# A fused S5 scan and GEGLU block on one core: another order for D's row, the parameters, C and slab 2 on the load queue

## The chip, the core and the metric

The kernel runs on one core of a Trainium2 chip. A core has five engines that run side by side: PE (TensorE, products of matrices), DVE (VectorE), ACT (ScalarE), POOL (GpSimd) and SP (SyncE, which here only issues transfers). The metric is the device time of one execution in microseconds (us). Four executions of the kernel before took 180.09 to 180.79 us, with a median of 180.47 us.

## The reference

```python
def reference(x, Lambda_re, Lambda_im, B_re, B_im, C_re, C_im, log_dt, Dskip, w_gate, w_up, w_down):
    xn = layernorm(x)                                   # x: 2048 x 512, bf16
    Lam = Lambda_re + 1j * Lambda_im                    # 512 states
    dt = exp(log_dt);  Lam_bar = exp(dt * Lam)
    B_bar = ((Lam_bar - 1) / Lam)[:, None] * (B_re + 1j * B_im)
    h_t = Lam_bar * h_{t-1} + B_bar @ xn_t              # over the 2048 tokens
    s = 2 * Re(h @ C.T) + xn * Dskip
    g = silu((gelu(xn @ w_gate) * (xn @ w_up)) @ w_down)    # w_gate, w_up: 512 x 1376
    return x + s * g
```

## The kernel before

The 2048 tokens are handled in four slabs of 512, and each slab in four tiles of 128 tokens. For every slab PE does four kinds of products: gate and up (`gate_tile`, line L530, for slabs 1 to 3, and `GatePair`, L501, for slab 0, where the 1376 columns come in three pieces as the weights land), the inputs of the scan (`inputs`, L638, against `BT`), the down product (`down_pair`, L573, against `wd`, with the gated activations turned by a DMA into `atT`), and the output of the scan (`y_tile`, L601, against `C2`).

Around them, ACT takes the results out of PSUM (`gt`, `ub`, `U`, `g`), with three table sets for its functions, and each change of set is an ACT_TABLE_LOAD. DVE multiplies gate and up into `at`, rotates the scan's inputs with tables of sines, runs the scan (TENSOR_TENSOR_SCAN, L675), and rotates back into `hst`. PSUM is cut into three slots of two banks (`slots`), which gate, up, inputs and down take in turn, and two single banks (`ybank`).

Every operation is first recorded as a step of a `Plan`, with an estimated cost and its dependencies. The plan then searches for an order and emits each engine's instructions in it. PE's steps are chained in the order of the program text; the other engines' steps may be moved by the planner, unless `after=` or `in_turn` ties them. Each engine then executes its own list strictly in order, and an instruction that waits holds up all that stand behind it.

Three places matter here.

The head. Small loads on ACT's queue bring three parameter vectors into `pv` and D's row (1 x 512) into `Drow[0:1]`. `dummies` are products of ones that keep PE busy. `columns` turns eight parameter rows into columns by one product with the identity (L393). `head_t(m)` turns the centred tile m of slab 0 on PE (L445), and ACT or DVE copies the result into `W` (L448, L449), which is the left operand of the first gate products. `spread` copies D's row to all 128 partitions: a product of one row of ones with `Drow[0:1]` (L748), and an ACT copy back into `Drow` (L749). `sines` makes the tables' sines (L705, L706). `damping` turns the third parameter vector with a product of its own (L739) and a DVE copy (L740).

The load queue. SP issues all large transfers. `dma_first` chains some of them; the rest stand where the planner puts them. In the kernel before, the order after slab 0's weights is: the transposing load of C's real part (L362), the transposition of slab 1 into `xnT` (L366), `wd` (L893), x of slab 2 (L872), the last rows of `wd` (L894), the transpositions of slab 0's `at` tiles 0 to 2 (L556), the transposing load of C's imaginary part (L362), `at` tile 3 (L556), and x of slab 3. Each `at` tile is turned into 11 blocks of `atT`, and the down product of tile m waits for the blocks of that tile.

C's scaling and slab 2's statistics. `tF` is C scaled by a coefficient on ACT (L897, four pieces), and DVE makes `C2` of it (L899, L902), which waits for both parts of C. Slab 2's mean and mean square are made on ACT (L876, eight steps), which waits for x of slab 2.

Of the kernel before, what the change touches and what calls it, by code (L numbers as in the profile page):

```python
# [202 lines left out]
def kernel(  # L203
# [46 lines left out]
    def sb(name, shape, dt=BF16):  # L250
        return consts.tile(shape, dt, name=name)
# [5 lines left out]
    wd = sb("wd", [P, NFT, D])  # L257
    BT = sb("BT", [P, 2, KT, D])
    C2 = sb("C2", [P, 2, NPT, D])
    pv = [sb("pv0", [2 * NPT, P]), sb("pv1", [NPT, P])]  # L260
    Drow = sb("Drow", [P, D])
    hst = [sb(f"hst{i}", [P, 2, NPT, TS]) for i in range(2)]
    CT = hst[1]
# [38 lines left out]
    def pe(n, cols, emit, reads=(), writes=(), **kw):  # L302
        return pl.add(PE, n * (cols + 6) / 2400.0, emit, reads, writes, lag=0.22, **kw)
# [4 lines left out]
    def dma(eng, issue, land, emit, reads=(), writes=(), **kw):  # L308
        return pl.add(eng, issue, emit, reads, writes, lag=land, **kw)
# [21 lines left out]
    def load_x(eng, q, m, land):  # L331
        dma_first(eng, 0.45, land, lambda: q.dma_start(out=x_tok[:, m, :], in_=x_r[:, m, :]), [("x", 0, m)], not_before=0.72)

    load_p(0, A_log_dt, pv[0][0:NPT, :])
    load_p(1, A_Lambda_im, pv[0][NPT : 2 * NPT, :])
    behind = [first[ACT]]
    load_p(2, A_Lambda_re, pv[1][:])
    dma(ACT, 0.4, 3.0, lambda: nc.scalar.dma_start(out=Drow[0:1, :], in_=A_Dskip.rearrange("(a d) -> a d", a=1)), writes=["Drow"], after=[first[ACT]], rank=-20.0)
    def load_first(c, which, land):
        load_w(dma_first, SP, nc.sync, c, (1.45 * (CH0[c][1] - CH0[c][0]) / 512, land), which)  # L340

# [19 lines left out]
    def load_c(ri):  # L361
        dma_first(SP, 1.9, 4.0, lambda: nc.sync.dma_start_transpose(out=CT[:, ri, :, :], in_=(A_C_re, A_C_im)[ri]), [("CT", ri)])  # L362

    def turn_slab(s, land, after=()):

# [20 lines left out]
    acts(1, lambda: act(out=tiny[:], in_=zero[:], func=AF.Exp), ["zero"], ["tiny"], table="exp", rank=150.0, after=behind)  # L386
    pf = small("pf", 16)
    dt_, thn, lim, lre = (pf[:, 4 * i : 4 * i + 4] for i in range(4))
    rows = slots[2][:, 0, 0 : 2 * NPT]

    def columns():

        pe(1, 150, lambda: T.matmul(rows, lhsT=pv[0][:], rhs=ident[0 : 2 * NPT, 0 : 2 * NPT], start=True, stop=True),  # L393
            [("pv", 0), ("pv", 1), "ident"], [("slot", 2, 0)])
        acts(4, lambda: act(out=dt_, in_=rows[:, 0:NPT], func=AF.Exp), [("slot", 2, 0), "tiny"], ["dt"], table="exp", rank=150.0)
# [123 lines left out]
    def gate_tile(s, m):  # L519
# [24 lines left out]
        for kind, (nm, wt, dst) in enumerate((("wg", wg, gt[q]), ("wu", wu, ub[q]))):  # L544
# [5 lines left out]
        dve(b - a, lambda: V.tensor_tensor(out=at[j][:, a:b], in0=gt[q][:, a:b], in1=ub[q][:, a:b], op=ALU.mult),  # L550
            [("gtb", q), ("ubb", q)], [("at", j, 2)], rate=2.0)

    def at_t(s, m, c0, c1):
        j = (s * M + m) % NAT
        k0, k1 = CK[c0][0], CK[c1][1]
        dma(SP, 1.3, 2.2, lambda: nc.sync.dma_start_transpose(  # L556
            out=atT[:, k0:k1, m * P : (m + 1) * P], in_=at[j][:, k0 * P : k1 * P]),
            [("at", j, c) for c in range(c0, c1 + 1)] + [("atpad", j)], [("atT", m, c) for c in range(c0, c1 + 1)])

    g2s = {}  # L560
    g2_n = [0]
# [142 lines left out]
    def sines():  # L704
        early.append(acts(196, lambda: act(out=sbt[:], in_=ang[:], func=AF.Sin, scale=TWO_PI), ["ang"], ["sbt"], table="silu", rank=20.0))  # L705
        early.append(acts(196, lambda: act(out=cbt[:], in_=kr[:], func=AF.Sin, scale=-TWO_PI, bias=halfpi[:]), ["kr", "halfpi"], ["cbt", "trig"], table="silu", rank=20.0))  # L706

    def tables(behind):
        NB4 = [P, NPT, NA, NB // 2, 2]
# [25 lines left out]

    def damping():

        ps = ybank[0][:, 0:NPT]
        pe(1, 150, lambda: T.matmul(ps, lhsT=pv[1][:], rhs=ident[0:NPT, 0:NPT], start=True, stop=True), [("pv", 2), "ident"], [("y", 0)])  # L739
        dve(4, lambda: V.tensor_copy(out=lre, in_=ps), [("y", 0)], ["lre"], base=0.14)  # L740
        dve(4, lambda: V.tensor_tensor(out=a1[:], in0=lre, in1=dt_, op=ALU.mult), ["lre", "dt"], ["a1"])
        power(rho[:], e_t[:], a1[:], 4, ["a1", "e_t"], ["rho"])

    def head_t(m, evict):
        return transposed(xc[m], xcT[:, m], [("xc", m), ("F", m // 2, m % 2)], [("xcT", m)], m % 2, evict)

    def spread():
        pe(1, 512, lambda: T.matmul(slots[2][:, 1, :], lhsT=warm[0:1, 0:P], rhs=Drow[0:1, :], start=True, stop=True), ["Drow", "warm"], [("slot", 2, 1)])  # L748
# [47 lines left out]
    pairs[2].products(1)  # L796
    pairs[3].products(0)
    pairs[3].products(1)
    gelus = [p.close() for p in pairs]
    tables(gelus[:1])  # L800
    load_rest()
# [10 lines left out]
        gate_pairs(m, 1)  # L812
    for h in range(2):
        half(0, h)
    for m in range(M):
# [44 lines left out]
    def norm1():  # L860
        for m in range(M):
            stats(1, m)
            mean(1, m)
        rstd(1, 0, M)
        for m in range(M):
            norm_dve(1, m)
        first[SP] = turn_slab(1, 3.0, [first[SP]])
        for m in range(M):
            skip(1, m)

    def norm_act(s):
        dma(SP, 0.5, 4.0, lambda: nc.sync.dma_start(out=x_tok[:, s * M : (s + 1) * M, :], in_=x_r[:, s * M : (s + 1) * M, :]),  # L872
            writes=[("x", s, m) for m in range(M)], not_before=(30.0, 50.0)[s - 2], rank=40.0)
        for m in range(M):
            for i, fn in enumerate((AF.Copy, AF.Square)):
                acts(512, lambda i=i, fn=fn, m=m: act(out=junk[:], in_=x_tok[:, s * M + m, :], func=fn, accum_out=sx[:, s, i, m : m + 1]),  # L876
                     [("x", s, m)], ["junk", ("sx", s, i, m)], ptr=2)
        mean, var = sx[:, s, 0, :], sx[:, s, 1, :]

        def f():  # L880
            V.tensor_scalar(out=mean, in0=mean, scalar1=1.0 / D, scalar2=None, op0=ALU.mult)
            V.tensor_tensor(out=mq[:, s, :], in0=mean, in1=mean, op=ALU.mult)
            V.tensor_scalar(out=var, in0=var, scalar1=1.0 / D, scalar2=EPS, op0=ALU.mult, op1=ALU.add)
            V.tensor_tensor(out=var, in0=var, in1=mq[:, s, :], op=ALU.subtract)
        pl.add(DVE, 0.35, f, [("sx", s, i, m) for i in range(2) for m in range(M)], [("var", s)], lag=0.13)
        power(rs[:, s, :], var, mhalf[:], M, [("var", s), "mhalf"], [("rs", s, m) for m in range(M)])
        dve(M, lambda: V.scalar_tensor_tensor(out=nb[:, s, :], in0=mean, scalar=-1.0, in1=rs[:, s, :], op0=ALU.mult, op1=ALU.mult),
            [("var", s)] + [("rs", s, m) for m in range(M)], [("nb", s)])
        for m in range(M):
            norm_out(s, m)  # L890

    norm1()
    dma_first(SP, 3.6, 4.3, lambda: nc.sync.dma_start(out=wd[:, 0 : NFT - 1, :], in_=B_w_down[0 : (NFT - 1) * P, :].rearrange("(k p) d -> p k d", p=P)), ["wd"])  # L893
    dma_first(SP, 0.4, 4.3, lambda: nc.sync.dma_start(out=wd[:FL, NFT - 1, :], in_=B_w_down[(NFT - 1) * P : F, :]), ["wd"])  # L894
    load_c(1)
    for pt in range(NPT):
        acts(1024, lambda pt=pt: act(out=tF[:, :, :], in_=CT[:, :, pt, :], func=AF.Copy, scale=cim[:, pt : pt + 1]),  # L897
             ["coef", ("CT", 0), ("CT", 1)], [("tF",)], ptr=1)
# [67 lines left out]
```

## Time and profile before

| what | value |
|---|---|
| four executions | 180.79, 180.19, 180.75, 180.09 us; median 180.47 us |
| the profiled execution | 180.79 us, of which 179.0 us are the span from the first to the last instruction |
| PE busy | 173.6 us (97% of the span), 852 products |
| DVE busy | 157.9 us (88%) |
| ACT busy | 119.3 us (67%) |
| POOL busy | 8.0 us (4%) |
| mean granted TensorE clock | 0.999 |
| moved by DMA | 18.53 MB, 104 GB/s on average |

The span leaves out some 1.8 us of the profiled execution (180.79 less 179.0). The table of forty slices (4.5 us each) shows PE at nine tenths or more from the second slice to the last but one, with a single 8 in the eleventh. DVE is as full from the fourth slice to the thirty-fourth. The DMA engines are full from the second slice to the tenth, that is to 45 us, and have pauses after the eleventh. Only the waits of the engine that sets the end cost time. A wait of one that is ahead costs nothing, until it makes that engine late.

### The profile page before, as it was taken

To read this page: it belongs to the slowest core of one execution; us is meant where nothing else is said; L and a number is where in the kernel's file an instruction comes from. 1 tells how busy PE (TensorE), PEld (TensorE's weight loads), DVE (VectorE), ACT (ScalarE), POOL (GpSimd) and SP (SyncE) were. 2 spreads that over 40 slices of the span, in tenths; PEclk is the share of its full clock that TensorE was granted. 3 is DMA by queue.
4 is the path that set the end of the run, shared out by engine and by line. 5 is a ranking of instruction groups with operands and counts; after the bars stand their busy time and mean duration, and the time that the engine had idled before them with its cause. 6 is when DMAs were issued, how large, how long until landed. Compare 5 with 4: busy or idle time off the path is not lost.

```text
span 179.0 us, 2401 instructions
## 1 busy us (share of the span) xinstructions
PE 173.6 (97%) x852; PEld 82.4 (46%) x852; DVE 157.9 (88%) x268; ACT 119.3 (67%) x180; POOL 8.0 (4%) x17
## 2 busy tenths in 40 slices
PE   7999999999899999999999999999999999999992
PEld 2454444444344445444445554544445555444451
DVE  4989999999999999999999999999999999860063
ACT  3899989678999988938259864554518666353220
POOL 2120023000002000000020000000000000000000
PEclk9999999999999999999999999999999999999999
DMA  5999999999700479400011665141100344420011
GB/s 144 322 243 209 310 114 190 354 232 216 118 0 0 84 139 140 81 29 2 0 59 36 111 135 105 36 81 33 60 0 0 72 82 93 97 72 29 0 58 59
DMA packets 49093, 18.53 MB, mean 104 GB/s; under 512 B 40409, under 2 KB 49082, under 8 KB 49082
## 3 DMA queue, kind: packets, MB, share of 16 engines
q1 hardware_dynamic: 49056, 18.39, 47.9%
q8 instruction: 6, 0.10, 0.2%
q14 instruction: 5, 0.04, 0.1%
q10 hardware_dynamic: 26, 0.00, 0.0%
HBM read 6.33 MB, written 2.10 MB: 47 GB/s over the span
## 4 chain that ended last, share of the span: by engine, by line
PE 70%; DVE 15%; DMA 8%; ACT 3%; SPq 1%; issue 1%; DVEq 0%
PE slot L530 31%; PE slot L573 17%; PE ybank L601 14%; PE slot L638 8%; DMA x_tok<-in_A_x_dram 4%; DMA atT<-at 3%; DVE Fs L675 3%; DVE Q L656 3%; DVE st L420 2%; DVE at L516 1%; DVE Q L725 1%; SPq L362 1%; DMA out_dram<-ot 1%; DVE sk L473 1%; DVE ot L606 1%
## 5 line engine op out<-in xcount | busy, mean ns | idle before, releaser
L530 PEld LDWEIGHTS <-xnT 128*128 128x128 bf16 x288 | 28.2, 98 | 28.4
L573 PE MATMUL slot<-wd,atT 128*128 128x512 bf16 (+1 forms) x176 | 38.9, 379 | 0.5 <-DMA atT<-at 0.5
L530 PE MATMUL slot<-wg,xnT 128*128 128x512 bf16 (+1 forms) x144 | 31.8, 357 | 0.0
L530 PE MATMUL slot<-wu,xnT 128*128 128x512 bf16 (+1 forms) x144 | 31.8, 357 | 0.0
L675 DVE TENSOR_TENSOR_SCAN Fs<-rho,ini,W 128x512 bf16<-128x512 f32 x24 | 29.3, 1267 | 0.1
L638 PE MATMUL slot<-xnT,BT 128*128 128x512 bf16 x128 | 28.6, 379 | 0.0
L601 PE MATMUL ybank<-C,hst 128*128 128x512 bf16 (+1 forms) x128 | 28.2, 372 | 0.0
L573 PEld LDWEIGHTS <-atT 128*128 128x128 bf16 (+1 forms) x176 | 17.1, 98 | 21.6 <-DMA atT<-at 1.0
L604 DVE TENSOR_TENSOR yg<-ybank,g 128x512 bf16<-128x512 f32 (+1 forms) x16 | 10.7, 668 | 12.7 <-PE ybank L601 12.6
L641 ACT ACTIVATE U<-slot 128x1024 bf16<-128x1024 f32 x16 | 16.0, 1017 | 8.0 <-PE slot L638 8.0
L577 ACT ACTIVATE g<-slot 128x1024 f32<-128x1024 f32 x8 | 8.2, 1023 | 17.3 <-PE slot L573 17.3
L601 PEld LDWEIGHTS <-hst 128*128 128x128 bf16 x136 | 13.3, 98 | 13.8
L638 PEld LDWEIGHTS <-BT 128*128 128x128 bf16 x128 | 12.5, 98 | 15.1
L656 DVE TENSOR_TENSOR Q<-U,tab 128x4096 bf16<-128x4096 bf16 x8 | 18.3, 2287 | 0.3
L656 DVE TENSOR_TENSOR Q<-Fs,tab 128x4096 bf16<-128x4096 bf16 x8 | 18.3, 2286 | 0.1
L538 ACT ACTIVATE gt<-slot 128x1024 bf16<-128x1024 f32 x12 | 12.3, 1024 | 7.1 <-PE slot L530 5.4
L597 ACT ACTIVATE ybank<-sk 128x512 f32<-128x512 bf16 (+1 forms) x16 | 9.3, 586 | 9.2 <-DVE yg L604 9.2
L538 ACT ACTIVATE ub<-slot 128x1024 bf16<-128x1024 f32 x12 | 12.3, 1023 | 3.3 <-PE slot L530 3.0
L876 ACT ACTIVATE junk<-x_tok 128x512 bf16<-128x512 bf16 x16 | 10.1, 628 | 1.5 <-DMA x_tok<-in_A_x_dram 1.3
L675 DVE TENSOR_TENSOR_SCAN Fs<-rho,W 128x512 bf16<-128x512 f32 x8 | 9.2, 1207 | 0.0
L548 DVE TENSOR_TENSOR at<-gt,ub 128x1024 bf16<-128x1024 bf16 x12 | 8.2, 685 | 0.3 <-ACT ub L538 0.2
L501 PEld LDWEIGHTS <-W 128*128 128x128 bf16 x64 | 5.9, 98 | 5.5 <-DVE W L449 0.3
(122 smaller groups left out, 182.4 us busy)
## 6 DMA issues: line engine op xcount, KB each, us to landing
out_dram<-ot SPq DMA_DIRECT2D x15, 128.0 KB, 1.7
x_tok<-in_A_x_dram SPq DMA_DIRECT2D x3, 512.0 KB, 6.0
wd<-in_B_w_down_dram SPq DMA_DIRECT2D x1, 1280.0 KB
x_tok<-in_A_x_dram SPq DMA_DIRECT2D x4, 128.0 KB, 2.8
wg<-in_B_w_gate_dram SPq DMA_DIRECT2D x1, 512.0 KB
wu<-in_B_w_up_dram SPq DMA_DIRECT2D x1, 512.0 KB, 6.5
wg<-in_B_w_gate_dram SPq DMA_DIRECT2D x1, 480.0 KB
wu<-in_B_w_up_dram SPq DMA_DIRECT2D x1, 480.0 KB, 7.8
```

The lines of the kernel that those rows point to most:

```text
L530: T.matmul(ps[:, bank, 0 : b - a], lhsT=xnT[s % 2][:, m, k, :], rhs=wt[:, k, a:b], start=(k == 0), stop=(k == KT - 1))
L538: acts(1024, lambda ps=ps, dst=dst, fn=fn: act(out=dst[:, 0:1024].rearrange("p (c w) -> p c w", c=2), in_=ps[:, :, :], func=fn), [("slot", ...
L548: dve(1024, lambda: V.tensor_tensor(out=at[j][:, 0:1024], in0=gt[q][:, 0:1024], in1=ub[q][:, 0:1024], op=ALU.mult), qs[0] + qs[1], [("at", ...
L573: T.matmul(ps[:, b, :], lhsT=atT[:fs, k, m * P : (m + 1) * P], rhs=wd[:fs, k, :], start=(k == 0), stop=(k == NFT - 1))
L597: acts(w, lambda: act(out=bank, in_=sk[s % 2][:, m, a:z], func=AF.Copy), [("sk", s % 2, m)], [key])
L601: T.matmul(bank, lhsT=hst[s % 2][:, j // NPT, j % NPT, m * P : (m + 1) * P], rhs=C2[:, j // NPT, j % NPT, a:z], start=False, stop=(j == 2 ...
L604: dve(w, lambda: V.tensor_tensor(out=yg[e][:, a:z], in0=bank, in1=g2[gi][:, b, a:z], op=ALU.mult), [key, ("g2", gi)], [("yg", e, a)], base ...
L638: T.matmul(ps[:, ri, :], lhsT=BT[:, ri, k, pt * P : (pt + 1) * P], rhs=xnT[s % 2][:, :, k, :], start=(k == 0), stop=(k == KT - 1))
L641: acts(1024, lambda q=q, ps=ps: act(out=U[ui][:, :, q, :], in_=ps[:, :, :], func=AF.Copy), [("slot", i, 0), ("slot", i, 1)], [("U", ui, q)])
L656: dve(4096, lambda: V.tensor_tensor(out=Qf, in0=src.unsqueeze(1).to_broadcast(WQ), in1=table, op=ALU.mult), reads, ["Q"], rate=2.0)
L675: pl.add(DVE, 1.116 if s == 0 else 1.19, lambda ri=ri, q=q, pt=pt, first=first: V.tensor_tensor_scan(out=Fs[:, ri, q, :], data0=rho[:, pt ...
L876: acts(512, lambda i=i, fn=fn, m=m: act(out=junk[:], in_=x_tok[:, s * M + m, :], func=fn, accum_out=sx[:, s, i, m : m + 1]), [("x", s, m)] ...
```

## The change

D's row is spread by a product over all 128 rows (`Drow` is set to zero first, then row 0 is loaded), placed between the first two PE transpositions in the stead of one of the dummies. All three parameter vectors lie in one tile and are turned by one product; `damping` keeps only its DVE and POOL steps, and is placed later in the text. C's imaginary part is loaded right behind the real part, ahead of slab 1's transposition. Slab 1's normalisation and `wd` stand earlier in the text. The `at` transpositions are tied to one another in order, and the load of x for slab 2 is tied between the first and the second of them. The sines are tied behind the copy of the third turned tile. The planner orders the rest anew.

```diff
-    pv = [sb("pv0", [2 * NPT, P]), sb("pv1", [NPT, P])]
+    pv = sb("pv", [3 * NPT, P])
...
-    load_p(0, A_log_dt, pv[0][0:NPT, :])
-    load_p(1, A_Lambda_im, pv[0][NPT : 2 * NPT, :])
-    behind = [first[ACT]]
-    load_p(2, A_Lambda_re, pv[1][:])
-    dma(ACT, 0.4, 3.0, lambda: nc.scalar.dma_start(out=Drow[0:1, :], in_=A_Dskip.rearrange("(a d) -> a d", a=1)), writes=["Drow"], after=[first[ACT]], rank=-20.0)
+    for i, v in enumerate((A_log_dt, A_Lambda_im, A_Lambda_re)):
+        load_p(i, v, pv[i * NPT : (i + 1) * NPT, :])
...
+    dve(256, lambda: V.memset(Drow[:], 0.0), writes=["Drow"], not_before=0.72, rank=275.0)
+    dma(ACT, 0.4, 2.5, lambda: nc.scalar.dma_start(out=Drow[0:1, :], in_=A_Dskip.rearrange("(a d) -> a d", a=1)), writes=["Drow"], after=[first[ACT]], rank=-20.0)
...
-        load_c(0)
+        for ri, src in enumerate((A_C_re, A_C_im)):
+            dma_first(SP, 1.9, 4.5, lambda ri=ri, src=src: nc.sync.dma_start_transpose(out=CT[:, ri, :, :], in_=src), [("CT", ri)])
...
-    rows = slots[2][:, 0, 0 : 2 * NPT]
+    rows = slots[0][:, 1, 0 : 3 * NPT]
...
-        pe(1, 150, lambda: T.matmul(rows, lhsT=pv[0][:], rhs=ident[0 : 2 * NPT, 0 : 2 * NPT], start=True, stop=True),
+        pe(1, 150, lambda: T.matmul(rows, lhsT=pv[:], rhs=ident[0 : 3 * NPT, 0 : 3 * NPT], start=True, stop=True),
...
-        dve(4, lambda: V.tensor_copy(out=lim, in_=rows[:, NPT : 2 * NPT]), [("slot", 2, 0)], ["lim"], base=0.14)
+        dve(8, lambda: V.tensor_copy(out=pf[:, 2 * NPT :], in_=rows[:, NPT:]), [("slot", 0, 1)], ["lim", "lre"], base=0.14)
...
     def at_t(s, m, c0, c1):
...
-        dma(SP, 1.3, 2.2, lambda: nc.sync.dma_start_transpose(
+        turned[s, m] = dma(SP, 1.3, 2.2, lambda: nc.sync.dma_start_transpose(
...
+            after=[turned[s, m - 1]] if m else [first[SP]] if s == 0 else [])
...
     def damping():
-        ps = ybank[0][:, 0:NPT]
-        pe(1, 150, lambda: T.matmul(ps, lhsT=pv[1][:], rhs=ident[0:NPT, 0:NPT], start=True, stop=True), [("pv", 2), "ident"], [("y", 0)])
-        dve(4, lambda: V.tensor_copy(out=lre, in_=ps), [("y", 0)], ["lre"], base=0.14)
...
     def spread():
-        pe(1, 512, lambda: T.matmul(slots[2][:, 1, :], lhsT=warm[0:1, 0:P], rhs=Drow[0:1, :], start=True, stop=True), ["Drow", "warm"], [("slot", 2, 1)])
+        pe(1, 512, lambda: T.matmul(slots[2][:, 1, :], lhsT=warm[:, 0:P], rhs=Drow[:], start=True, stop=True), ["Drow", "warm"], [("slot", 2, 1)])
...
-    dummies(1, 0)
+    dummies(1, 1)
...
     head_t(0, ACT)
-    dummies(2, 0)
+    dummies(1, 1)
+    spread()
     behind = [head_t(1, ACT)]
...
-    sines()
...
     pairs[0].products(0)
-    spread()
     pairs[1].products(0)
     pairs[0].products(1)
-    head_t(2, ACT)
+    sines([head_t(2, ACT)])
     pairs[1].products(1)
-    damping()
...
     pairs[3].products(1)
+    damping()
...
     for h in range(2):
         half(0, h)
+    norm1()
+    dma_first(SP, 3.6, 4.3, lambda: nc.sync.dma_start(out=wd[:, 0 : NFT - 1, :], in_=B_w_down[0 : (NFT - 1) * P, :].rearrange("(k p) d -> p k d", p=P)), ["wd"])
+    dma_first(SP, 0.4, 4.3, lambda: nc.sync.dma_start(out=wd[:FL, NFT - 1, :], in_=B_w_down[(NFT - 1) * P : F, :]), ["wd"])
+    def load_slab(s, after=()):
+        return dma(SP, 0.5, 4.0, lambda: nc.sync.dma_start(out=x_tok[:, s * M : (s + 1) * M, :], in_=x_r[:, s * M : (s + 1) * M, :]),
+            writes=[("x", s, m) for m in range(M)], not_before=(30.0, 50.0)[s - 2], after=after)
     for m in range(M):
         gate_pairs(m, 2)
         at_t(0, m, 0, 2)
+        if m == 0:
+            turned[0, 0] = load_slab(2, [turned[0, 0]])
...
-    norm1()
...
-    load_c(1)
```

In the changed kernel as built, SP's list after the real part of C reads: imaginary part of C, slab 1's transposition, `wd`, the last rows of `wd`, `at` tile 0, x of slab 2, `at` tiles 1, 2 and 3, x of slab 3. ACT's list at the start of the down product reads: two copies `U`, three of slab 2's statistics, two copies `U`, the first `tF`, five statistics, the second `tF`, a table load, both `g`, a table load, the first `gt` of slab 1. On DVE, two of slab 0's four 512 wide `at` products stand ahead of slab 1's statistics in the kernel before and one in the changed kernel; the fourth of them stands just ahead of the first rotation there.

More of the change, by code (lines that the diff above doesn't have):

```diff
@@ L332, in load_x @@
         dma_first(eng, 0.45, land, lambda: q.dma_start(out=x_tok[:, m, :], in_=x_r[:, m, :]), [("x", 0, m)], not_before=0.72)
-    load_p(0, A_log_dt, pv[0][0:NPT, :])
-    load_p(1, A_Lambda_im, pv[0][NPT : 2 * NPT, :])
-    behind = [first[ACT]]
-    load_p(2, A_Lambda_re, pv[1][:])
-    dma(ACT, 0.4, 3.0, lambda: nc.scalar.dma_start(out=Drow[0:1, :], in_=A_Dskip.rearrange("(a d) -> a d", a=1)), writes=["Drow"], after=[first[ACT]], rank=-20.0)
+    behind = []
+    for i, v in enumerate((A_log_dt, A_Lambda_im, A_Lambda_re)):
+        load_p(i, v, pv[i * NPT : (i + 1) * NPT, :])
+        if i == 1:
+            behind = [first[ACT]]
+    dve(256, lambda: V.memset(Drow[:], 0.0), writes=["Drow"], not_before=0.72, rank=275.0)
+    dma(ACT, 0.4, 2.5, lambda: nc.scalar.dma_start(out=Drow[0:1, :], in_=A_Dskip.rearrange("(a d) -> a d", a=1)), writes=["Drow"], after=[first[ACT]], rank=-20.0)
     def load_first(c, which, land):
@@ L358, in load_rest @@
             load_w(dma_first, SP, nc.sync, 2, (1.35, 3.5), which)
-        load_c(0)
-    def load_c(ri):
-        dma_first(SP, 1.9, 4.0, lambda: nc.sync.dma_start_transpose(out=CT[:, ri, :, :], in_=(A_C_re, A_C_im)[ri]), [("CT", ri)])
+        for ri, src in enumerate((A_C_re, A_C_im)):
+            dma_first(SP, 1.9, 4.5, lambda ri=ri, src=src: nc.sync.dma_start_transpose(out=CT[:, ri, :, :], in_=src), [("CT", ri)])
     def turn_slab(s, land, after=()):
@@ L388 @@
     dt_, thn, lim, lre = (pf[:, 4 * i : 4 * i + 4] for i in range(4))
-    rows = slots[2][:, 0, 0 : 2 * NPT]
+    rows = slots[0][:, 1, 0 : 3 * NPT]
     def columns():
-        pe(1, 150, lambda: T.matmul(rows, lhsT=pv[0][:], rhs=ident[0 : 2 * NPT, 0 : 2 * NPT], start=True, stop=True),
-            [("pv", 0), ("pv", 1), "ident"], [("slot", 2, 0)])
-        acts(4, lambda: act(out=dt_, in_=rows[:, 0:NPT], func=AF.Exp), [("slot", 2, 0), "tiny"], ["dt"], table="exp", rank=150.0)
+        pe(1, 150, lambda: T.matmul(rows, lhsT=pv[:], rhs=ident[0 : 3 * NPT, 0 : 3 * NPT], start=True, stop=True),
+            [("pv", 0), ("pv", 1), ("pv", 2), "ident"], [("slot", 0, 1)])
+        acts(4, lambda: act(out=dt_, in_=rows[:, 0:NPT], func=AF.Exp), [("slot", 0, 1), "tiny"], ["dt"], table="exp", rank=150.0)
     def turn_angles():
-        dve(4, lambda: V.tensor_copy(out=lim, in_=rows[:, NPT : 2 * NPT]), [("slot", 2, 0)], ["lim"], base=0.14)
+        dve(8, lambda: V.tensor_copy(out=pf[:, 2 * NPT :], in_=rows[:, NPT:]), [("slot", 0, 1)], ["lim", "lre"], base=0.14)
         dve(4, lambda: V.tensor_tensor(out=thn, in0=lim, in1=dt_, op=ALU.mult), ["lim", "dt"], ["thn"])
@@ L551, in gate_tile @@
             [("gtb", q), ("ubb", q)], [("at", j, 2)], rate=2.0)
+    turned = {}
     def at_t(s, m, c0, c1):
@@ L555, in at_t @@
         k0, k1 = CK[c0][0], CK[c1][1]
-        dma(SP, 1.3, 2.2, lambda: nc.sync.dma_start_transpose(
+        turned[s, m] = dma(SP, 1.3, 2.2, lambda: nc.sync.dma_start_transpose(
             out=atT[:, k0:k1, m * P : (m + 1) * P], in_=at[j][:, k0 * P : k1 * P]),
-            [("at", j, c) for c in range(c0, c1 + 1)] + [("atpad", j)], [("atT", m, c) for c in range(c0, c1 + 1)])
+            [("at", j, c) for c in range(c0, c1 + 1)] + [("atpad", j)], [("atT", m, c) for c in range(c0, c1 + 1)],
+            after=[turned[s, m - 1]] if m else [first[SP]] if s == 0 else [])
     g2s = {}
@@ L702, in angle, with sines @@
             dve(196, lambda: V.scalar_tensor_tensor(out=kr[:], in0=ang[:], scalar=-1.0, in1=ang[:], op0=ALU.mult, op1=ALU.max), ["ang"], ["kr"], base=0.13)
-    def sines():
-        early.append(acts(196, lambda: act(out=sbt[:], in_=ang[:], func=AF.Sin, scale=TWO_PI), ["ang"], ["sbt"], table="silu", rank=20.0))
-        early.append(acts(196, lambda: act(out=cbt[:], in_=kr[:], func=AF.Sin, scale=-TWO_PI, bias=halfpi[:]), ["kr", "halfpi"], ["cbt", "trig"], table="silu", rank=20.0))
+    def sines(behind):
+        early.append(acts(196, lambda: act(out=sbt[:], in_=ang[:], func=AF.Sin, scale=TWO_PI), ["ang"], ["sbt"], table="silu", rank=20.0, after=behind))
+        early.append(acts(196, lambda: act(out=cbt[:], in_=kr[:], func=AF.Sin, scale=-TWO_PI, bias=halfpi[:]), ["kr", "halfpi"], ["cbt", "trig"], table="silu", rank=20.0, after=behind))
     def tables(behind):
@@ L814, with norm1 @@
         half(0, h)
+    def norm1():
+        for m in range(M):
+            stats(1, m)
+            mean(1, m)
+        rstd(1, 0, M)
+        for m in range(M):
+            norm_dve(1, m)
+        first[SP] = turn_slab(1, 3.0, [first[SP]])
+        for m in range(M):
+            skip(1, m)
+    norm1()
[4 more added lines that the diff above has]
+            writes=[("x", s, m) for m in range(M)], not_before=(30.0, 50.0)[s - 2], after=after)
     for m in range(M):
@@ L858, in norm_out @@
         dma(SP, 1.2, 1.3, lambda: nc.sync.dma_start_transpose(out=xnT[s % 2][:, m, :, :], in_=xn[m]), [("xn", m)], [("xnT", s % 2, m)])
[L860 to L869, printed above, removed]
     def norm_act(s):
-        dma(SP, 0.5, 4.0, lambda: nc.sync.dma_start(out=x_tok[:, s * M : (s + 1) * M, :], in_=x_r[:, s * M : (s + 1) * M, :]),
-            writes=[("x", s, m) for m in range(M)], not_before=(30.0, 50.0)[s - 2], rank=40.0)
+        if s > 2:
+            load_slab(s)
         for m in range(M):
@@ L890, in norm_act @@
             norm_out(s, m)
-    norm1()
-    dma_first(SP, 3.6, 4.3, lambda: nc.sync.dma_start(out=wd[:, 0 : NFT - 1, :], in_=B_w_down[0 : (NFT - 1) * P, :].rearrange("(k p) d -> p k d", p=P)), ["wd"])
-    dma_first(SP, 0.4, 4.3, lambda: nc.sync.dma_start(out=wd[:FL, NFT - 1, :], in_=B_w_down[(NFT - 1) * P : F, :]), ["wd"])
-    load_c(1)
     for pt in range(NPT):
```

## The prediction

> **What bounds the kernel now.** I read first what PE waited for, since the page gives it 97% of the span. The columns are the engine, its line, what it waited for, us in total, times, longest.
>
> ```profile
> engine line waited for: us in total, times, longest us
> PE slot L437 <- DVE zero L381: 1.1, 1, 1.1
> PE slot L573 <- DMA atT<-at: 0.5, 1, 0.5
> PE ybank L445 <- DVE Fs L466: 0.2, 1, 0.2
> ```
>
> The reader is to see that PE sets the end by itself. After the start there is one wait of size in the whole run, in the first down product, for the transposition of tile 3 of `at`. Its true size is larger than 0.5: PE's timeline starts the 33 down products of tiles 0 to 2 at 39.33 and the 11 of tile 3 at 47.16. At the pace of the inputs before them (32 products from 32.42 to 39.33, 0.216 each) tile 3 would start at 39.33 + 33 x 0.216 = 46.46. So the stall is 0.70 us; the end of PE's busy time is modelled and covers a part of it. The four executions are two near 180.77 and two near 180.14, 0.63 apart. I take it, as an inference, that the stall is in two of the four. The profiled execution is one of those that have it.
>
> Next I read SP's timeline, to see why the tile is late. The columns are start, duration on the queue, and the transfer.
>
> ```profile
> 17.52 6.79 SPq L362 DMA_TRANSPOSE hst<-in_A_C_re_dram  x1
> 26.06 1.91 SPq L366 DMA_TRANSPOSE xnT<-xn  x1
> 28.02 1.02 SPq L893 DMA_DIRECT2D wd<-in_B_w_down_dram  x1
> 29.08 0.69 SPq L872 DMA_DIRECT2D x_tok<-in_A_x_dram  x1
> 29.81 0.50 SPq L894 DMA_DIRECT2D wd<-in_B_w_down_dram  x1
> 31.31 7.74 SPq L556 DMA_TRANSPOSE atT<-at  x3
> 39.10 2.26 SPq L362 DMA_TRANSPOSE hst<-in_A_C_im_dram  x1
> 41.45 1.63 SPq L556 DMA_TRANSPOSE atT<-at  x1
> ```
>
> Tile 3 of `at` was ready on DVE at 36.8 (L516, 36.39 + 0.38), and left at 41.45, behind C's imaginary part. It landed at 47.12, 5.66 later by the chain of waits. From 24.31 to 26.06 the queue was idle.
>
> Third, ACT's timeline, since ACT empties the PSUM slots that PE takes next. The bracket is the idle time ahead.
>
> ```profile
> 36.68 0.63 ACT L876 ACTIVATE junk<-x_tok 128x512 bf16<-128x512 bf16 x1 [1.31 <-DMA x_tok<-in_A_x_dram]
> ...
> 44.09 1.15 ACT L897 ACTIVATE tF<-hst,cim 128x1024 f32<-128x1024 bf16 x1 [0.47 <-DMA hst<-in_A_C_im_dram]
> ...
> 52.09 1.02 ACT L538 ACTIVATE gt<-slot 128x1024 bf16<-128x1024 f32 x1
> ```
>
> The first `gt` of slab 1 leaves its slot at 53.11, and PE takes that slot again at 54.20, after the stall. So ACT had 1.09 us to spare, and without the stall it would have 0.4.
>
> Last the head.
>
> ```profile
> 5.92 0.60 ACT L448 ACTIVATE W<-ybank 128x512 bf16<-128x512 bf16 x1 [0.46 <-PE ybank L445]
> ...
> 6.46 0.39 PE L748 MATMUL slot<-Drow,junk 1*128 1x512 bf16 x1
> ...
> 6.78 1.09 PEld L501 LDWEIGHTS <-W 128*128 128x128 bf16 x8 [0.23 <-ACT W L448]
> ...
> 9.16 0.16 PE L739 MATMUL ybank<-ident,pv 4*128 4x4 bf16 x1
> ```
>
> The row's product lies in a gap: PE goes on at 6.78 only when the second turned tile is out of PSUM.
>
> **The Trainium skill.** "TensorE: Matmul & The Clock Gate", section "Wait — 56ns, not 53.3ns?", gives 426.7 ns from start to start for 512 columns cold and 215.7 warm. The trace agrees: the six dummies' weight loads stand 0.43 apart, the warm pace is 0.216. The price is by columns, so I take 128 rows to cost what one row costs. "DMA: Bandwidth & Descriptors", section "Queues, rings and completion order", says that each DMA engine consumes descriptors in ring order. This agrees: `at` tile 0, behind 1.9 MB of loads, needed 6.9 us from issue to landing, against a median of 3.5. "ScalarE: Activation LUTs", section "What ACT_TABLE_LOAD costs", gives 1283 ns and a drain of 1380 ns; the trace has 1.28, and the next instruction follows at once, so I count no drain. "VectorE: DVE Perf Modes", section "Zero memsets can be issued as uint32 (trn2)", prices a memset at one cycle per element. I use it once, below.
>
> **The head, part by part.** Setting `Drow` to zero is one memset of 256 words. None of that width is in the trace; 128 elements took 0.17, and 128 more cycles at 0.96 GHz are 0.13, so 0.3 as an estimate. DVE waits for x until 2.92, and D's load is issued at 1.95, so both hide it. The price is 0, at worst 0.1 if the load waited; behind it on ACT stands the first table load, at 2.25, which nothing needs before 3.95.
>
> The product with 12 parameter rows now waits for the third vector, too. The second, issued at 1.31, had landed by 3.73. The third is issued 0.29 later, so at worst the product starts at 4.02. The first turned tile moves by as much at most, and the first gate product with it, but PE is idle from 6.37 to 6.78 in any case once D's product is gone from there. Price 0.
>
> D's product (0.216) replaces a dummy ahead of the second turned tile, which DVE releases at 5.42. PE has time from 4.87 to 5.48, so D's row must land by 5.48 - 0.22 = 5.26, 3.3 us after its issue. The first x tile needed 2.15, the first weights 3.6. I take 0; the bounds are 0 and about 1 us (weights' latency and a queue of its own). ACT's copy of the row (0.49 from its start to the next) moves from 7.93 to between the first and second `W` copies: 5.46 + 0.49 = 5.95, while the second `W` starts at 5.92 now. Price 0.03.
>
> What goes at 6.46 and 9.16 gives nothing at 6.46 (the gap stays). At 9.16 PE is idle from 8.95 until the third `W` copy ends at 9.11, and that copy starts at 8.51 because PE's turned tile ends at 8.48. So at most 0.1 is won. It is lost again at 12.13, where PE takes the first slot, which `gt` empties at 12.06. `damping` loses a DVE copy (0.07); its product of 0.09 moves into the head's DVE list, so the angles are ready at 8.54 and not 8.44, for sines that start at 9.01. Its power on POOL goes ahead of slab 1's, into time when POOL is idle (11 to 23 us). The head sums to 0, with 0.1 to 0.3 of gain as the upper bound (the whole idle time at 9 us) and 1 us of loss as the lower one.
>
> **The load queue.** C's imaginary part (2.26 on SP) goes at 24.35 into the idle 1.75. SP is free at 26.6, DVE has slab 1 ready at 26.3 (26.0 + 0.33, since one `at` product of 0.33 moves behind the statistics that wait for x until 20.13). Slab 1's transposition so leaves at 26.65, 0.6 later, and lands after 4.5 (as now) at 31.2; PE needs it at 32.4. Next `wd` at 28.6 and its rest at 29.7. Ahead of `at` tile 0 lie 1.376 MB, no longer 1.9. At 0.345 MB per us (the trace in windows of 1 us, from 32 to 36) they take 4.0 us from about 30.4, to 34.4; tile 0 then takes 1.6 and 0.6 to its receipt: 36.6, where PE needs it at 39.1 and had it at 38.2. x of slab 2 follows, 0.512 MB in 1.5 us, landing at **38.1**, 1.4 later than now. Tile 1 lands near 40 (needed 41.5), tile 2 near 41.5 (43.9). Tile 3 is multiplied later on DVE, behind the rotation (2.2), at 39.1, and lands at 43 to 44; PE needs it at 46.3. So the stall of **0.70** goes, with 2 us to spare.
>
> **What is late next.** ACT's list puts three statistics behind slab 2's x, so ACT idles from 37.0 to L = 38.1, and the two `U` behind them wait too. From L, with the times from start to start in the trace: three statistics 2.13, two `U` 1.80, `tF` 1.05, five statistics 3.65, `tF` 1.06, table load 1.29, `g` 0.92, `g` 1.04, table load 1.30, `gt` 1.02: 15.26, plus 0.05 to PE. PE, no longer stalled, wants the slot at 54.20 - 0.71 = 53.49. That is met if L is at most **38.18**. A second condition: the second `tF` overwrites what two DVE products read. The second of them ran from 46.03 to 46.77 and moves by at most 0.2, to 46.95. From there 1.06 + 1.29 + 0.92 + 1.04 + 1.30 + 1.02 + 0.05 give 53.63, 0.14 after PE's wish. I take the new stall as 0.15. It is the same ACT chain that the stall used to hide.
>
> Behind that point the order of ACT and DVE changes too, but PE had no wait there, and ACT is half idle from 80 us on. Slab 1's `C2` is complete near 62, for 63.1. I count 0; the bounds are -0.1 and +0.5.
>
> **Sum.** Against the profiled execution: 180.79 - 0.70 + 0.15 = 180.24. Against the median of 180.47 it is 0.2 less, as only half the runs seem to have the stall. The span would be 178.45. I forecast 180.2, less than a measurement of this kernel can tell from no change, which is about 0.3%, 0.54 us.
>
> **Rivals.** (1) Nothing takes the stall's place and the head gives its idle time, too: 180.79 - 0.70 - 0.3 = 179.8. For it: PE's gap near 9 us is real, and the ACT copy of D's row leaves the third `W` copy's way. Against it: PE's own tile ends at 8.48. Chance 0.28. (2) Slab 2's x lands late behind `at` tile 0, on the same rings, and ACT's chain holds PE in the first gate tile of slab 1: each us of L beyond 38.18 is a us lost, and from L = 39.1 the kernel is slower by over 0.3%. At L = 39.3, 180.79 - 0.70 + 1.15 = 181.2. For it: x of slab 2 took 7.6 us from issue now. Against it: 0.5 MB less lies ahead of tile 0. Chance 0.18. (3) D's row lands after 5.26 and holds the second turned tile, and all of PE and ACT behind it: 180.24 + 1 = 181.2. Chance 0.06. (4) The stall stays, as the same bytes move through full DMA engines: 180.7. Chance 0.03. The first case keeps 0.45, of which 0.02 fall below 179.93.
>
> Faster: 0.28 + 0.02 = 0.30. Within: 0.43 + 0.03 = 0.46. Slower: 0.18 + 0.06 = 0.24. The likeliest case alone reaches from 179.9 to 180.8. The range of 179.5 to 181.4 takes in the bounds of the head and of L up to 39.5.
>
> **What would show it.** No wait of L573 for `atT`; C's imaginary part issued near 24.4; slab 2's x landing near 38; a wait of L530 for ACT `gt` of 0 to 0.3 near 53.5; PE starting the products on the second turned tile at 6.78 as now. I am wrong if PE waits for the DMA of `Drow`, if L530 waits a us or more, or if the first gate products start earlier.

## The result, and the profile after

The changed kernel takes 181.11 us (median of 43 runs, 180.13 to 182.5), the kernel before 180.42 (median of 64 runs, 180.02 to 181.67). The ratio is 1.0039, 95% interval 1.0029 to 1.0050: slower by 0.7 us. The forecast was 180.2 (range 179.5 to 181.4), no measurable change.

The execution that was profiled took 180.06 us, less than any of the 43. So its profile shows what the change does when all goes well. A second profiled execution of the same kernel took 181.03, close to the median. The two are read side by side here, as "the quick" and "the typical" execution.

What PE waited for in the quick execution (engine, line, what it waited for, us in total, times, longest):

```profile
PE slot L437 <- DVE junk L379: 1.1, 1, 1.1
PE slot L501 <- ACT W L448: 0.3, 1, 0.3
```

The wait for the transposition of tile 3 of `at` is gone, and nothing behind the head takes its place. The same in the typical execution:

```profile
PE slot L437 <- DVE junk L379: 1.1, 1, 1.1
PE slot L530 <- ACT g L580: 0.5, 1, 0.5
PE slot L530 <- ACT gt L538: 0.2, 1, 0.2
```

PE now waits twice in slab 1's first gate tile, for slots that ACT has not emptied. SP's timeline of the quick execution (start, duration on the queue, line, transfer) shows the new order of the queue:

```profile
17.38 5.82 SPq L362 DMA_TRANSPOSE hst<-in_A_C_re_dram  x1
23.25 2.27 SPq L362 DMA_TRANSPOSE hst<-in_A_C_im_dram  x1
25.62 2.49 SPq L366 DMA_TRANSPOSE xnT<-xn  x1
28.16 0.58 SPq L826 DMA_DIRECT2D wd<-in_B_w_down_dram  x1
28.79 0.68 SPq L827 DMA_DIRECT2D wd<-in_B_w_down_dram  x1
31.01 2.21 SPq L558 DMA_TRANSPOSE atT<-at  x1
33.27 0.59 SPq L830 DMA_DIRECT2D x_tok<-in_A_x_dram  x1
33.96 6.29 SPq L558 DMA_TRANSPOSE atT<-at  x3
```

C's imaginary part stands in the time that was idle. x of slab 2 leaves at 33.27, where it left at 29.08 before. Now ACT's timeline around the landing of that x (the bracket is the idle time ahead), first the quick execution, then the typical one:

```profile
37.96 0.63 ACT L885 ACTIVATE junk<-x_tok 128x512 bf16<-128x512 bf16 x1 [0.85 <-DMA x_tok<-in_A_x_dram]
...
52.27 1.02 ACT L538 ACTIVATE gt<-slot 128x1024 bf16<-128x1024 f32 x1
```

```profile
39.05 0.63 ACT L885 ACTIVATE junk<-x_tok 128x512 bf16<-128x512 bf16 x1 [1.77 <-DMA x_tok<-in_A_x_dram]
...
53.39 1.02 ACT L538 ACTIVATE gt<-slot 128x1024 bf16<-128x1024 f32 x1
```

The landing L of slab 2's x is 37.96 in one and 39.05 in the other, 1.09 later. The first `gt` of slab 1 starts 1.12 later, and the time is 0.97 longer. All of ACT's list between the two rows has moved as one block. PE's timeline has the products that take that `gt`'s slot next (first the quick, then the typical execution):

```profile
53.49 1.89 PE L530 MATMUL slot<-wg,xnT 128*128 128x512 bf16 x8
```

```profile
54.47 1.89 PE L530 MATMUL slot<-wg,xnT 128*128 128x512 bf16 x8 [0.17 <-ACT gt L538]
```

They start 0.98 later, and that is the whole difference between the two executions.

### The profile page after: what moved, and what is told of

Its sections match the earlier page's. It is cut to its first block, busy times and chain, and to the rows that moved or that the text cites. A ratio compares the mean times of both kernels' runs of the same rounds, so it can differ in the third digit from the quotient of the medians.

```text
span 178.3 us, 2398 instructions
## 1 busy us (share of the span) xinstructions
PE 173.4 (97%) x850; PEld 82.5 (46%) x850; DVE 157.9 (89%) x268; ACT 119.2 (67%) x180; POOL 7.9 (4%) x17
## 4 chain that ended last, share of the span: by engine, by line
PE 95%; DVE 1%; DMA 1%; ACT 1%; issue 0%; DVEq 0%
PE slot L530 31%; PE slot L576 21%; PE slot L641 15%; PE ybank L604 14%; PE slot L501 9%; PE slot L437 2%; PE ybank L501 2%; DMA out_dram<-ot 1%; DVE ot L609 1%; DVE yg L607 1%; PE ybank L445 0%; ACT Drow L749 0%; ACT W L448 0%; PE slot L748 0%; DVE junk L379 0%
## 5 line engine op out<-in xcount | busy, mean ns | idle before, releaser
L530 PEld LDWEIGHTS <-xnT 128*128 128x128 bf16 x288 | 28.2, 98 | 28.4
L530 PE MATMUL slot<-wu,xnT 128*128 128x512 bf16 (+1 forms) x144 | 31.8, 357 | 0.0
L530 PE MATMUL slot<-wg,xnT 128*128 128x512 bf16 (+1 forms) x144 | 31.8, 357 | 0.0
L641 PE MATMUL slot<-xnT,BT 128*128 128x512 bf16 x128 | 28.6, 379 | 0.0
L641 PEld LDWEIGHTS <-BT 128*128 128x128 bf16 x128 | 12.5, 98 | 15.1
```

Of the source, the lines that this page charges most:

```text
L530: T.matmul(ps[:, bank, 0 : b - a], lhsT=xnT[s % 2][:, m, k, :], rhs=wt[:, k, a:b], start=(k == 0), stop=(k == KT - 1))
L641: T.matmul(ps[:, ri, :], lhsT=BT[:, ri, k, pt * P : (pt + 1) * P], rhs=xnT[s % 2][:, :, k, :], start=(k == 0), stop=(k == KT - 1))
```

## The experiments

Three theories. **X** is the prediction's rival 2: x of slab 2 lands late behind tile 0, and ACT's list, which stands still until x is there, holds PE in slab 1's first gate tile. **C**: C's imaginary part ahead of slab 1's transposition costs as much as it brings. **D**: the loss lies in the head, where ACT's copy of D's row now stands ahead of the second `W` copy, or is no more than scatter. In each experiment only the named list of one engine differs, or of two in experiment 3, and of three in experiment 9, which joins 2 and 3; all other lists are those of the kernel it starts from. Line numbers shift by a few, so that L530 is L537 to L539 there. Each is compared with runs of the kernel before beside it on the same chip: their median was 180.42 us for experiments 1 to 4, and 180.72 for the others, of which 5, 6, 8 and 9 ran on a second chip and 7 on a third. Beside these experiments the changed kernel itself ran on the first chip only (experiment 1), so experiments of different chips are best compared by their ratios.

**1. The changed kernel again** (no edit).

> The changed kernel unaltered, for another profiled execution and its spread on this chip. Theory X (x of slab 2 lands late in most executions and ACT's chain then holds PE in the first gate tile of slab 1): median near 181.1, and where the profiled execution is at 180.8 or more, PE waits for ACT in L530 near 50 to 54 us. Theory D (D's row lands late): PE waits for the DMA of Drow or starts the products on the second turned tile after 6.8. Theory C (slab 1's transposition lands late behind C's imaginary part): PE waits in L641 near 32.4.

Measured: 181.33 us (22 runs), ratio 1.0051 (1.0030 to 1.0071). This is the typical execution above. The loss repeats, and it has a place: 0.5 + 0.2 us of waits for `g` and `gt`, with x at 39.05. Theory C's sign, a wait in L641, did not come. Of theory D's signs one came in small: the weights for the products on the second turned tile are loaded at 6.92, where it was 6.79 in the quick execution, behind ACT's copies; PE did not wait for the DMA of D's row.

**2. x of slab 2 ahead of tile 0.**

```
 SP:  wd, wd's rest
+SP:  x of slab 2
 SP:  at tile 0
-SP:  x of slab 2
 SP:  at tiles 1, 2, 3
```

> The changed kernel with one transfer moved in SP's list: x of slab 2 ahead of at tile 0 instead of behind it. All other lists are the same. Theory X: x lands some 1.5 us earlier, the time falls to 180.1 to 180.4. Theories D and C: no change, near 181.1.

Measured: 180.22 us (14 runs), ratio 0.9992 (0.9976 to 1.0009). The loss is gone. On ACT's timeline the first statistic has no bracket, since x is there before ACT is, and the second `tF` now waits for DVE's product and not for ACT's own list:

```profile
37.21 0.63 ACT L894 ACTIVATE junk<-x_tok 128x512 bf16<-128x512 bf16 x1
...
46.28 1.15 ACT L911 ACTIVATE tF<-hst,cim 128x1024 f32<-128x1024 bf16 x1 [0.34 <-DVE C L916]
...
52.00 1.02 ACT L545 ACTIVATE gt<-slot 128x1024 bf16<-128x1024 f32 x1
```

One transfer, one place further ahead on its queue, accounts for the loss as far as the interval can tell. That speaks for X.

**3. D's product of 128 rows late.**

```
-PE:   D's product ahead of the second turned tile
+PE:   D's product behind the first gate product
-ACT:  copy of D's row ahead of the second W copy
+ACT:  copy of D's row behind the second table load, ahead of the third W copy
```

> The changed kernel with D's product (still 128 rows) back behind the first gate product and its ACT copy back ahead of the third W copy; no dummy takes its place. All other lists are the same. Theory D: the time falls to 180.2 to 180.5. Theories X and C: no change, near 181.1.

Measured: 180.97 us (22 runs), ratio 1.0038 (1.0024 to 1.0052). Still slower than before, so D is not the main cause. It is 0.36 us less than experiment 1 on the same chip, but the intervals overlap; a part of that size is neither shown nor excluded by the medians. Its profiled execution (181.47 us) has the latest x of the four profiled with this queue order, and the longest wait for `g`:

```profile
39.47 0.63 ACT L895 ACTIVATE junk<-x_tok 128x512 bf16<-128x512 bf16 x1 [2.38 <-DMA x_tok<-in_A_x_dram]
```

```profile
PE slot L537 <- ACT g L587: 1.1, 1, 1.1
```

From 37.96 to 39.47 are 1.51 of L, and from 180.06 to 181.47 are 1.41 of time: 0.93 us for each us of L.

**4. C's imaginary part late.**

```
 SP:  C real
-SP:  C imaginary
 SP:  slab 1's xnT, wd, wd's rest, at tile 0, x of slab 2, at tiles 1, 2
+SP:  C imaginary
 SP:  at tile 3
```

> The changed kernel with the load of C's imaginary part moved in SP's list from behind the real part to behind at tile 2, where it was before. All other lists are the same. Theory C: near 180.3. Theory X: x of slab 2 lands about 2 us earlier, but tile 3 and tF wait for the late C as before: 180.2 to 180.8. Theory D: no change, near 181.1.

Measured: 181.92 us (6 runs: four from 181.71 to 181.94, two near 185.1, on which see the last section), ratio without those two 1.0072 (1.0050 to 1.0095). Slower yet, so C falls. The band given for X was missed as well: x left at 33.54, since it still stands behind tile 0, and landed at 38.52, half a us and not 2 us before the typical execution. And C's late landing now stops ACT a second time, at the first `tF`, and the stall of tile 3 is back:

```profile
43.91 1.15 ACT L912 ACTIVATE tF<-hst,cim 128x1024 f32<-128x1024 bf16 x1 [1.33 <-DMA hst<-in_A_C_im_dram]
```

```profile
PE slot L584 <- DMA atT<-at: 0.3, 1, 0.3
```

The added wait of 1.33 puts ACT's list where an x at some 39.9 would have put it (38.52 + 1.33), and PE waits 1.2 for the first `g`. This fits X's chain, but the expectation had not counted it.

**5. x of slab 2 still later** (the dose).

```
 SP:  at tile 0
-SP:  x of slab 2
 SP:  at tile 1
+SP:  x of slab 2
 SP:  at tiles 2, 3
```

> The kernel after, with one move: x of slab 2 goes on SP's queue behind the transposition of `at` tile 1, not behind that of tile 0. Theory X (ACT's chain from the landing L of slab 2's x holds PE in slab 1's first gate tile; a us of L is a us of time): one transposition of some 2.3 us on SP more lies ahead, so L goes from 38 to 39.5 to some 40 to 42, and the time from 181.1 to 182.5 or more, with waits of PE for `g` and `gt` of 2 us together. Theory D (the time is lost in the head, or to run-to-run noise of the runs compared): 181.1, unchanged.

Measured: 185.30 us (6 runs), ratio 1.0223 (1.0168 to 1.0278). The sign is that of X; the size is larger. The waits of PE, and the chain of waits in order of time (start, us, what):

```profile
PE slot L537 <- ACT g L587: 2.5, 1, 2.5
PE slot L583 <- ACT U L651: 0.7, 1, 0.7
```

```profile
36.16 1.24 SPq L565
37.40 0.05 issue
37.45 4.47 DMA x_tok<-in_A_x_dram
41.92 0.02 issue
41.95 0.73 ACT junk L895 x2
```

The end is set by SP's queue, then x's transfer, then ACT from its first statistic on. x is 3.99 later than in the quick execution and the time 5.19 longer (185.25 against 180.06). The waits are 3.2 of it. A further 1.7 come from PE's clock, see the last section.

**6. Two statistics moved behind slab 1's first gate tile on ACT** (SP as in the changed kernel).

```
 ACT:  first tF, three statistics
-ACT:  two statistics
 ACT:  second tF, g, g, gt, ub, ub (352 wide)
+ACT:  two statistics
 ACT:  gt (352 wide)
```

> The kernel after, with every queue's list unchanged, x of slab 2 in its late place; on ACT alone the last two of slab 2's statistics (2 x 0.755 us) go from ahead of the second `tF` to behind the four copies of slab 1's first gate tile. Theory X: what counts is ACT's chain and not the transfer itself. With L = 39.05, the chain is 1.4 shorter (then the second `tF` waits for DVE at 46.3), `gt` ends at 53.0, ahead of PE's wish at 53.6, so the waits for `g` and `gt` go, and the time comes to 180.2 to 180.4. If the loss has nothing to do with ACT's chain, it stays at 181.1. If later copies are held by the moved statistics instead, it lies between.

Measured: 181.83 us (22 runs), ratio 1.0060 (1.0039 to 1.0081). The expected gain did not come, and the time lies above all three cases. The two statistics stand ahead of the tile's last copy, the `gt` of 352 columns, and not behind it as the expectation has it. x came at 39.32.

```profile
47.51 1.15 ACT L915 ACTIVATE tF<-hst,cim 128x1024 f32<-128x1024 bf16 x1 [0.98 <-DVE C L920]
```

```profile
PE slot L539 <- ACT gt L547: 0.9, 2, 0.7
PE slot L539 <- ACT g L589: 0.3, 1, 0.3
```

Of the 1.5 us taken out, 0.98 are spent waiting for DVE, whose product comes behind the first `tF` and so behind x as well. The moved work then holds a `gt` slot for which PE waits 0.7 at 59.84. This does not tell X from its rivals. In this order ACT had no room to give between x and 60 us.

**7. x in the same place of the queue as in 5, but not at the head of ACT's list.**

```
 (SP as in experiment 5)
-ACT:  three statistics of slab 2
 ACT:  U, U, first tF
+ACT:  three statistics of slab 2
 ACT:  five statistics, second tF
```

> The kernel x2_late (x of slab 2 behind `at` tile 1 on SP, 185.3 us), with its queues unchanged; on ACT alone the first three statistics of slab 2 go from ahead of the two `U` copies to behind the first `tF`. Theory X, in the form that what costs is the in-order wait for x at the head of ACT's list: `U` (40.4) and `tF` (41.2, when DVE has the coefficients) no longer wait for x, the eight statistics then run from 42.3 to 48.3, the second `tF` to 49.4, `g` to 52.6, `gt` to 54.9, where PE wants its slot at 53.6. So PE loses some 1.3 and not 5, and the time is 181.3 to 181.8, although x lands at 42 as in x2_late. Rival: the late transfer itself, or what it shares the DMA engines with, costs the time: 184 to 185.5.

Measured: 181.57 us (10 runs), ratio 1.0046 (1.0023 to 1.0069), against 185.30 in experiment 5. The queue's order is the same; x leaves SP at 36.75, where it left at 37.45 in experiment 5, and lands 4.1 later, near 40.9. That is 1.1 earlier than in experiment 5, but still 1.4 later than the latest x of the changed order. On ACT the first `tF` waits only for DVE's coefficient, and the first statistic waits for nothing:

```profile
41.68 1.15 ACT L917 ACTIVATE tF<-hst,cim 128x1024 f32<-128x1024 bf16 x1 [1.27 <-DVE cim L874]
42.73 0.61 ACT L897 ACTIVATE junk<-x_tok 128x512 bf16<-128x512 bf16 x1
```

```profile
PE slot L537 <- ACT g L587: 1.6, 1, 1.6
PE slot L537 <- ACT gt L545: 0.2, 1, 0.2
```

So the rival falls: x lands later than in any profiled execution of the changed order, no engine waits for it, and the ratio is about that of the changed kernel. But not all of the 3.3 us between the two profiled executions (185.25 and 181.98) is won by ACT's order. With the old order an x at 40.9 would have had `gt` start near 55.2 (as an estimate, L + 14.3 as in the quick execution); it started at 54.32. So some 0.8 are the order, 1.1 the earlier landing, and the rest PE's clock, which did not fall here. What a late x costs, it costs through the instruction that waits for it, ahead of `U`, `tF`, `g` and `gt` on an engine that runs its list in order.

**8. The kernel before, with C's imaginary part ahead** (that part of the change alone).

```
 SP:  C real
+SP:  C imaginary
 SP:  slab 1's xnT, wd, x of slab 2, wd's rest, at tiles 0, 1, 2
-SP:  C imaginary
 SP:  at tile 3
```

> The kernel before, in its own planned order on every engine, with one move on SP's queue: C's imaginary part goes right behind the real part, so that tile 3 of `at` has nothing ahead of it. x of slab 2 keeps its place ahead of `wd`'s rest. Theory X: the part of the change that moves C brings what the prediction gave it, the stall ahead of tile 3's down products (0.7 where it occurs) goes, x lands at 37 to 37.7 and nothing takes its place: 180.0 to 180.2, on average 0.3 under the kernel before. Theory C (C ahead costs as much as it brings, since x and `wd` start later): 180.4 to 181.1.

Measured: 180.33 us (22 runs), ratio 0.9968 (0.9949 to 0.9986): faster than the kernel before, by 0.39 us between the medians. It lies between the two bands, above X's and just below C's; beside the 180.72 of the kernel before, C ahead brings more than it costs. x leaves at 30.27 and lands at 37.66. PE's timeline has the down product in one piece, and the gate tile follows without a wait:

```profile
39.35 9.67 PE L581 MATMUL slot<-wd,atT 128*128 128x512 bf16 x43
48.86 1.67 PE L538 MATMUL slot<-wg,xnT 128*128 128x512 bf16 x7
50.59 1.89 PE L538 MATMUL slot<-wu,xnT 128*128 128x512 bf16 x8
```

**9. A version against both: experiments 2 and 3 together.**

> The kernel after, with x of slab 2 ahead of `at` tile 0 on SP's queue and D's product of 128 rows back behind the first gate product (ACT's copy of it behind the second table load). Theory X with nothing else of weight: 180.0 to 180.2, since the second `W` copy starts at 5.9 and not at 6.15 to 6.27, which gives 0.0 to 0.2 at the start of the down products, and PE waits nowhere behind them. If the early product is worth having: 180.3 or more.

Measured: 180.46 us (22 runs), ratio 0.9968 (0.9948 to 0.9989). Against the kernel before it gains as much as experiment 8, and it keeps the parts of the change that were not tried alone (the parameters' one product, `damping`, the sines), so these cost nothing that shows together. Its second `W` copy starts at 5.79 and its down product at 39.25. By the letter of the expectation 180.46 speaks for the early product. But the kernel before is 0.3 slower on this chip than on that of experiment 2, and the intervals of experiments 2 and 9 overlap, so what the head contributes is not settled by the medians.

## Why the prediction was wrong

**The cause is rival 2**, which got a chance of 0.18. Experiments 2, 5 and 7 show it: x earlier takes the loss away, x later makes it larger, and with ACT's list no longer standing behind it an x later still costs no more than the change itself.

**The step that failed** is "tile 0 then takes 1.6 and 0.6 to its receipt: 36.6" with what hangs on it, "x of slab 2 follows, 0.512 MB in 1.5 us, landing at 38.1", and the use of that landing as one value with 0.08 us to spare. Four executions with this order on SP have L at 37.96, 39.05, 39.32 (experiment 6) and 39.47 (experiment 3). The forecast hit the first of them, which is a lucky draw: that execution was faster than all 43 timed runs. The three others are 0.9 to 1.4 us later than forecast. With 0.93 us of time for each us of L, the median of 181.11 corresponds to L near 39.1 (37.96 + 1.05/0.93).

The term that was too small is mostly the one ahead of x. By its issue and its time to landing, tile 0 was there at 36.2 in the quick execution (31.0 + 5.2), at 37.4 in the typical one (31.0 + 6.4), and at 37.1 and 37.9 in experiments 6 and 3, where 36.6 was counted. x came 1.5 to 2.2 behind it, where 1.5 was counted. In the typical execution tile 0 makes 0.8 of the 0.95 us. A small slip is in the sum as well: the sizes are in units of 1024 bytes and the rate in units of 1000, which is 0.13 us over both loads, more than the 0.08 to spare.

Why tile 0 is late is less clear. I let everything flow at 0.345 MB per us, the rate of plain loads alone. From the table by windows (window, granted clock, busy time of the engines with the number of instructions, DMA share, GB/s), the quick execution and then the typical one:

```profile
34.00:35.00 1.00, 1.00 (x6) 0.43 (x5) 1.00 (x2) 0.65 (x1) 0.00 (x0) 1.00 1.24 214
35.00:36.00 1.00, 1.00 (x6) 0.49 (x5) 1.00 (x2) 0.37 (x1) 0.00 (x0) 1.00 1.29 320
```

```profile
35.00:36.00 1.00, 1.00 (x6) 0.47 (x5) 1.00 (x2) 0.55 (x1) 0.00 (x0) 1.00 1.63 169
36.00:37.00 1.00, 1.00 (x7) 0.47 (x5) 1.00 (x2) 0.75 (x1) 0.00 (x0) 1.00 0.74 166
```

Where tile 0 is being turned, the rate falls to 214 for one window in the one and to 169 and 166 for two in the other. Over the eight windows from 29 to 37 the quick execution moved 2.30 MB and the typical one 1.93 MB. The 0.37 MB between them are 1.07 us at 345, about the 1.09 between the two landings. That the turning itself slows the load is my reading of these rows; no run isolates it. The queue may have a part: x stands behind tile 0's own time on SP (2.21, 2.61, 2.73 and 3.00 in the four executions), it left at 33.27, 33.70, 34.28 and 34.36, and it landed in the same order. But all four left well before 36.6, from where the forecast lets its bytes flow, so that the later issue made the later landing is not shown.

A third thing I overlooked: PE asks for the slot of the first `g` before that of `gt`. It takes it at 51.22 in the typical execution, L + 12.17, and wants it at 50.57 in the quick one, so the limit there is L = 38.4. From start to start 0.47 us are lost there and 0.35 at `gt`. That moves the place of the loss and not its size: `gt`'s slot comes at L + 15.4 either way.

**What held, step by step.**

- The stall of 0.70: gone, as predicted. Experiment 8 prices this part alone at 0.32% (0.14 to 0.51%), 0.6 us of 180.72, or 0.4 between the medians. The inference that the stall is in two of four executions of the kernel before is neither confirmed nor refuted: its 64 runs lie between 180.02 and 181.67 without two heaps.
- The sum for L = 38.1 was 180.24; the execution with L = 37.96 took 180.06. The mechanism and the length of ACT's chain were right: from L to `gt`'s end are 15.33 in the quick execution and 15.36 in the typical one, against 15.26. PE goes on at L + 15.42 in the typical execution, so that the limit of 38.18 was 38.07 (53.49 - 15.42).
- The second condition (the second `tF` waits for DVE, so `gt` is free at 53.63) did not bind in the quick execution: DVE's product started at 45.54, not at 46.03 or later, and `gt` ended at 53.29. In experiment 9, with x at 37.88, `tF` waits 0.33 for DVE, `gt` ends at 52.63 + 1.02 = 53.65, and PE goes on at 53.71, some 0.3 later than without a wait.
- The head: the copy of D's row goes ahead of the second `W` copy, as said. I had the copy at 5.46 and the price at 0.03. ACT's timeline of the typical execution:

```profile
5.78 0.60 ACT L749 ACTIVATE Drow<-slot 128x512 bf16<-128x512 f32 x1 [0.26 <-PE slot L748]
6.27 0.59 ACT L448 ACTIVATE W<-ybank 128x512 bf16<-128x512 bf16 x1
```

The copy waits for D's product, which at the pace of the start (the dummies stand 0.43 apart) took 0.36 in the quick and 0.42 in the typical execution, and not 0.216. In experiment 3, where it comes later, its 128 rows took 0.22, as the one row was taken to cost. The second `W` copy starts at 6.15 (quick) and 6.27 (typical), not at 5.95. Much of it falls into PE's gap. The down product starts at 39.12 to 39.54 in the seven profiled executions with the early product (39.33 quick, 39.51 typical) and at 39.25 to 39.35 in the four without. So the head costs PE's start 0.2 at most and in some executions nothing; where PE waits for ACT later, as in the typical execution, this adds nothing to the time; rival 3, a late row that takes 1 us, did not occur.

- Slab 1's transposition left at 25.62 (26.65 predicted), C's imaginary part at 23.25 (24.35), since C's real part held the queue for 5.82 and not 6.79. Both only made room.

**The chances.** The profile had a chain with 0.08 us to spare and a transfer whose time from issue to landing was already 7.6 us in a busy queue. From L = 39.1 on the kernel is slower by over 0.3%, and that is 1.0 us from the forecast. I gave it 0.18, as if L were known to better than a us, from a single execution.

## What to carry to other kernels

Before a load is moved back on its queue, look at what stands behind its first reader on that engine: not the reader's due time but that of all the instructions behind it is the load's due time. A landing read from one execution is one draw; where a chain has less spare time than such draws differ (here 1.5 us), cost the late case and not the middle. Changes that travel together should be priced one by one: here one move won 0.4 to 0.6 us, and another in the same edit lost more than that.

## What the runs showed of the hardware

A wait of PE can cost more than itself. In experiment 5 PE stood idle for 2.52 us, and then its products ran at half pace (PE's timeline):

```profile
54.09 3.13 PE L537 MATMUL slot<-wu,xnT 128*128 128x512 bf16 x8 [2.52 <-ACT g L587]
57.01 1.25 PE L537 MATMUL slot<-wg,xnT 128*128 128x352 bf16 x4
58.09 0.76 PE L537 MATMUL slot<-wu,xnT 128*128 128x352 bf16 x4
```

From start to start, eight products of 512 columns took 2.92 and not 1.73, four of 352 took 1.08 and not 0.59: 1.7 us on top of the wait. The granted clock was 0.57 from 54 to 58 and 1.00 in the windows on both sides. The other executions agree: of the six, five had a mean clock of 0.991 and took 184.78 to 186.02 us, and one had 1.000 and took 183.64. The two runs of experiment 4 near 185.1 had 0.991, too; they were not profiled, and their waits are not known. A wait of 1.62 in experiment 7 was followed by the normal pace (1.73 for the eight). "TensorE: Matmul & The Clock Gate", section "What's actually happening", in the Trainium skill describes a gate that slows the clock when PE idles, after at least one idle window of some 3.4 us. Here the slow stretch followed 2.52 us of idle time; that the wait set it off is my reading of this one profile and of the six clocks.
